# The first batch of a fused attention and feed-forward kernel: division by a product with diagonals, products with v in another PSUM bank, weight conversion moved behind the row maxima, and earlier starts of the feed-forward part

## The chip, the cores and the metric

The kernel runs on one core of one Trainium2 chip. The metric is the device time of one execution in microseconds. Times are medians of three or more executions. "The profile" is one profiled execution; its span is about 1.8 us shorter than the device time of the same execution.

In the lines of the profile PE is TensorE, PEld its weight loads, DVE VectorE, ACT ScalarE and POOL GpSimd. A line of a timeline gives the start and the length in us, the engine, the line of the kernel, the operation and its tiles; in brackets stands how long the engine was idle before it, and what ended that. A line of waits gives the total in us, the number of waits and the longest. The granted clock is the share of full speed that TensorE was given in a stretch. "To turn" weights means to transpose them in blocks of 128x128; the rest is the last 64 of the 576 keys.

## The reference, cut to what matters

```python
scores = scale * np.matmul(q, k.transpose(0, 1, 3, 2))        # 8 batches, 8 heads, 576 x 576
thresh = np.max(scores, axis=-1, keepdims=True) - tau
scores = np.where(scores >= thresh, scores, -1000000000.0)
attn = np.exp(scores - np.max(scores, axis=-1, keepdims=True))
attn = attn / (np.sum(attn, axis=-1, keepdims=True) + 1e-09)
attn_out = np.matmul(attn, v)                                 # -> x, 8 x 576 x 512
...
xn = (x - mu) / np.sqrt(var + 1e-06) * g_ln
out = x + np.maximum(xn @ w_ch1, 0.0) @ w_ch2                 # 512 -> 2048 -> 512
```

The two weight matrices arrive as 64-bit floats and are turned into 32-bit ones on the chip.

## The kernel before

The program issues 72 slots of attention, nine for each batch. A slot takes two heads and 256 of their 576 rows (the fifth slot takes the rest of all heads). Each slot has four quarters, at which pieces of other work are issued between the attention's own. Sixteen groups of 288 tokens go through the feed-forward part; the first can start when the first five slots are done.

Beside the first slots, 32 chunks of the weights are converted. One call of `tick` ends one chunk, carries the next, and begins a third. VectorE and ScalarE begin, GpSimd carries, VectorE ends.

```python
def tick(self):
    self.ticks += 1
    if self.ended < self.carried and self.due[self.ended] <= self.ticks:
        self.end()        # VectorE L266, then GpSimd L271 (scale by g)
    if self.carried < self.begun:
        self.carry()      # GpSimd L257
    if self.begun < self.fetched:
        self.begin()      # VectorE L239, L243; ScalarE L247, L251
```

The attention of a slot, with the division on GpSimd and, in the first batch, the turning on TensorE:

```python
def weights(es, thr):
    den = small.tile([128, 4], F32, tag="den", name="den")
    for i in range(4):
        nc.vector.scalar_tensor_tensor(                       # L389
            out=es[:, i], in0=blocks[i], scalar=thr[:, i : i + 1], in1=es[:, i],
            op0=ALU.is_ge, op1=ALU.mult, accum_out=den[:, i : i + 1],
        )
    nc.vector.reciprocal(den, den)
    for i in range(4):
        nc.gpsimd.tensor_scalar(                              # L395
            out=es[:, i], in0=es[:, i], scalar1=den[:, i : i + 1], scalar2=1.0, ...
        )

def turn_weights(s, es):
    em, er = turned_tiles(s)
    for i in range(4):
        if i == 2:
            yield
        tp = ps_ff.tile([128, J, 128], F32, tag="ff", name="tp")   # this pool has two PSUM buffers
        for c in range(J):
            nc.tensor.transpose(tp[:, c], es[:, i, c * 128 : (c + 1) * 128], ident)
        ...                                                   # ScalarE copies tp to em
    tr = ps_ff.tile([64, 4, 128], F32, tag="ff", name="tr")
    ...                                                       # the last 64 keys, copied to er
```

The loop over the slots, cut to the order of issue:

```python
pv = sc[0][:, 2 * S : 2 * S + QH]          # products with v: behind the scores, in their tile
...
for n in range(NS):
    b, s = divmod(n, SLOTS)
    ticks = (0, 2, 3) if n < 6 else range(5)
    tick(0)
    scores(b, s)                           # TensorE
    run(n, -1)                             # first half of turning the slot before
    rest = exponentials()                  # VectorE: maxima (L372); ScalarE: exponentials
    es, thr = next(rest)
    run(n, 0)                              # second half of turning
    ...
    tick(1); run(n, 1)
    weights(es, thr)
    tick(2); run(n, 2); tick(3)
    ...
    run(n, 3)                              # products with v of the slot before
    tick(4)
```

Of the kernel before, what the change touches and what calls it, by code (L numbers as in the profile page):

```python
# [8 lines left out]
F32 = mybir.dt.float32  # L9
# [9 lines left out]
def kernel(  # L19
# [31 lines left out]
    nc = tc.nc  # L51
    B, H, S, D = q.shape
# [3 lines left out]
    HP = H // 2  # L56
    NK = DM // 128
    ND = DF // 128
    J = 4
    NB = S // 32  # L60
    TOK = S // 2
    QH = 256
# [11 lines left out]
    ffn = ctx.enter_context(tc.tile_pool(name="ffn", bufs=2))  # L74
    ps_sc = ctx.enter_context(tc.tile_pool(name="ps_sc", bufs=1, space=bass.MemoryType.PSUM))
    ps_ff = ctx.enter_context(tc.tile_pool(name="ps_ff", bufs=2, space=bass.MemoryType.PSUM))
# [6 lines left out]
    ident = consts.tile([128, 128], F32, name="ident")  # L83
# [11 lines left out]
    def product(out, lhsT, rhs, **flags):  # L95


        for h in range(2):
            r = slice(64 * h, 64 * h + 64)
            nc.tensor.matmul(out[r], lhsT=lhsT[:, r], rhs=rhs, **flags)  # L100
# [20 lines left out]
    def load_v(u):  # L121
# [13 lines left out]
        out=tau_sb, in_=bass.AP(tensor=tau.tensor, offset=tau.offset, ap=[[0, 128], [1, 1]])  # L135
    )
    load_qk(0, (nc.sync, nc.scalar))
    for t in q_diag + rests + v_rest:
# [9 lines left out]
        out=scl_sb, in0=tau_sb, scalar1=0.0, scalar2=SCALE, op0=ALU.is_ge, op1=ALU.mult  # L148
    )
    nc.vector.tensor_scalar(  # L150
        out=low_sb, in0=tau_sb, scalar1=0.0, scalar2=BIG, op0=ALU.is_lt, op1=ALU.mult
    )
    nc.vector.scalar_tensor_tensor(
        out=low_sb, in0=tau_sb, scalar=-1.0, in1=low_sb, op0=ALU.mult, op1=ALU.subtract
# [5 lines left out]
    class Weights:  # L160
# [116 lines left out]
# [3 lines that stand above are left out]
                self.end()  # L280
            if self.carried < self.begun:
                self.carry()
            if self.begun < self.fetched:
                self.begin()

    def by_blocks(u):

        return units[u][0] > 0
# [33 lines left out]


    sc = [ps_sc.tile([128, 3 * 512], F32, name=f"sc{i}") for i in range(2)]
    pv = sc[0][:, 2 * S : 2 * S + QH]
    blocks = [sc[i // 2][:, i % 2 * S : i % 2 * S + S] for i in range(4)]

    def span(at, n):
# [53 lines left out]
                yield es, thr  # L382
            nc.scalar.activation(es[:, i], blocks[i], func=AF.Exp, bias=neg[:, i : i + 1])  # L383

    def weights(es, thr):

        den = small.tile([128, 4], F32, tag="den", name="den")
        for i in range(4):
            nc.vector.scalar_tensor_tensor(  # L389
                out=es[:, i], in0=blocks[i], scalar=thr[:, i : i + 1], in1=es[:, i],  # L390
                op0=ALU.is_ge, op1=ALU.mult, accum_out=den[:, i : i + 1],
            )
        nc.vector.reciprocal(den, den)  # L393
        for i in range(4):
            nc.gpsimd.tensor_scalar(  # L395
                out=es[:, i], in0=es[:, i], scalar1=den[:, i : i + 1], scalar2=1.0,
                op0=ALU.mult, op1=ALU.mult,
            )



# [3 lines left out]
    def turned_tiles(s):  # L405
        return att.tile([128, J, 4, 128], F32, tag="em", bufs=1, name="em"), rests[s % 2]

    def turn_weights(s, es):

        em, er = turned_tiles(s)  # L410
        for i in range(4):
            if i == 2:
                yield
            tp = ps_ff.tile([128, J, 128], F32, tag="ff", name="tp")
            for c in range(J):
                nc.tensor.transpose(tp[:, c], es[:, i, c * 128 : (c + 1) * 128], ident)
            if s == HP:
                nc.scalar.copy(
                    em[:, :, :, 32 * i : 32 * i + 32], tp.rearrange("p c (a x) -> p c a x", a=4)
                )  # L420
            else:
                h, j = divmod(i, 2)
                nc.scalar.copy(  # L423
                    em[:, :, 2 * j : 2 * j + 2, 64 * h : 64 * h + 64],
                    tp.rearrange("p c (a x) -> p c a x", a=2),
                )
        tr = ps_ff.tile([64, 4, 128], F32, tag="ff", name="tr")
        for i in range(4):
            nc.tensor.transpose(tr[:, i], es[:, i, 512:576], ident)  # L429
        if s == HP:  # L430
            nc.scalar.copy(
                er[:64].rearrange("p a (u x) -> p u a x", u=HP),
                tr.rearrange("p u (a x) -> p u a x", a=4),
            )
        else:
            nc.scalar.copy(
                er[:64].rearrange("p a (h x) -> p h a x", h=2),
                tr.rearrange("p (h j) (a x) -> p h (j a) x", h=2, a=2),
            )
        yield em, er  # L440
# [38 lines left out]
    def values_of(b, s, turned_weights):  # L479

        em, er = turned_weights
        if s == HP:
            outs = [(hp, pv[:, hp * 64 : hp * 64 + 64]) for hp in range(HP)]
            pick = lambda t, hp, h: t[:, 2 * h : 2 * h + 2, hp * 32 : hp * 32 + 32]
        else:
            outs = [(s if s < HP else s - HP - 1, pv)]
            pick = lambda t, hp, h: t[:, :, 64 * h : 64 * h + 64]
        for hp, dst in outs:
            vt, vr = values_in[b * HP + hp]
            for c in range(J + 1):  # L490
                for h in range(2):
                    nc.tensor.matmul(  # L492
                        dst[64 * h : 64 * h + 64],
                        lhsT=vt[:, c, h, :] if c < J else vr[:, h, :],
                        rhs=pick(em[:, c] if c < J else er, hp, h),
                        start=(c == 0), stop=(c == J),
                    )
        if s == HP:
            for t in range(2):
                nc.scalar.copy(  # L500
                    x_of(2 * b + t)[:, :, QH:],
                    pv.rearrange("p (u t x) -> p t u x", u=HP, t=2)[:, t],
                )
                for c in range(1, NK):
                    add_feature(2 * b + t, c, slice(QH, TOK))
        else:
            g = 2 * b + (s > HP)
            hp = outs[0][0]
            nc.scalar.copy(x_of(g)[:, hp, :QH], pv)  # L509
            if hp:  # L510
                add_feature(g, hp, slice(0, QH))
# [30 lines left out]
    def run_all(calls):  # L542
        now = calls[:]
        calls.clear()
        for fn in now:
            fn()
# [79 lines left out]
    def at_quarter(n, i, fn, *args):  # L626
        later_calls.setdefault((n, i), []).append((fn, args))
# [4 lines left out]

    def ready(g):

        b, t = divmod(g, 2)
        return QUARTERS * (b * SLOTS + (HP, 2 * HP)[t] + 2) + (2, 4)[t]

# [42 lines left out]
    load_v(1)  # L680
    for n in range(NS):
        b, s = divmod(n, SLOTS)
        ticks = (0, 2, 3) if n < 6 else range(5)

        def tick(i):
            if i in ticks:
                conversion.tick()

        tick(0)
        scores(b, s)  # L690
        run(n, -1)
        rest = exponentials()
        es, thr = next(rest)
        run(n, 0)
        conversion.fetch(2)
        run_all(stores)
        second_part(n, 0)
        next(rest, None)

        u = (n + 1) // SLOTS * HP + (n + 1) % SLOTS  # L700
        if (n + 1) % SLOTS < HP and u < len(units):
            turn(u)
            if u + 1 < len(units):
                load_qk(u + 1)
        run_all(aside)
        tick(1)
        run(n, 1)
        second_part(n, 1)
        weights(es, thr)
        run_all(aside)  # L710
        run_all(stores)
        tick(2)
        run(n, 2)
        second_part(n, 2)
        tick(3)
        box = []
        if by_blocks(b * HP):
            scr = turn_blocks(s, es)
            at_quarter(n + 1, 0, lambda s=s, scr=scr, box=box: box.append(fetch(s, scr)))
        else:  # L720
            made = turn_weights(s, es)
            at_quarter(n + 1, -1, next, made)
            at_quarter(n + 1, 0, lambda made=made, box=box: box.append(next(made)))
        at_quarter(n + 1, 3, lambda b=b, s=s, box=box: values_of(b, s, box[0]))
        if s in (HP, 2 * HP):
            group_ready(2 * b + (s > HP))
        run_all(aside)
        conversion.fetch(2)
        run(n, 3)
        if b == 0 and s < HP - 2:  # L730
            load_v(s + 2)
        elif n >= SLOTS - 2 and (n + 2) % SLOTS < HP and n < NS - 2:
            load_v((n + 2) // SLOTS * HP + (n + 2) % SLOTS)
        second_part(n, 3)
        tick(4)
        run_all(aside)
    while later_calls or queue or aside or stores:
        n += 1
        for i in range(QUARTERS):
            run(n, i)  # L740
            second_part(n, i)
            run_all(aside)
            run_all(stores)
# [30 lines left out]
```

## Time and profile before

The time before is 1529.1 us (four executions, 1528.78 to 1529.36). The stretches of the span:

| stretch, us | TensorE busy, us | granted clock |
|---|---|---|
| 0 to 30 | 9.54 | 0.77 |
| 30 to 134 (attention of slots 1 to 6 and conversion) | 56.45 of 104 | 0.75 |
| 134 to 212 (slots 6 to 9, first feed-forward group) | 65.59 of 78 | 0.87 |
| 212 to 290 | 75.52 of 78 | 0.99 |

After that TensorE is busy at full clock nearly all the time.

### The profile page before, as it was taken

The page shows a single profiled execution, that of the slowest core. Times are in us where ns is not written, and L with a number is a line of the kernel's source. Part 1 is how long each engine was busy: PE and PEld are TensorE (multiplying, and loading weights), DVE is VectorE, ACT ScalarE, POOL GpSimd, SP SyncE. Part 2 cuts the span into 40 slices and gives each one's busy share as a digit, 9 for nine tenths or more (in the row PEclk, how much of TensorE's full clock was granted, in tenths as well). Part 3 has the DMA queues.
Part 4 walks back from the last instruction along what each step waited for, and adds up shares of the span by engine and source line. Part 5 has one row for each costly group of instructions (what it writes and reads, how often), then busy time and mean ns, then how long its engine had stood idle before and what let it go on. Part 6 is the DMA issues. An engine that isn't in the chain of part 4 may idle for free.

```text
span 1527.7 us, 28886 instructions
## 1 busy us (share of the span) xinstructions
PE 1416.8 (93%) x11700; PEld 833.7 (55%) x11700; DVE 837.7 (55%) x1380; ACT 442.2 (29%) x797; POOL 487.7 (32%) x737
## 2 busy tenths in 40 slices
PE   3557899999999999999999999999999999999998
PEld 1335455565555555565555655565555655565554
DVE  5877855555654566455664556455654556545210
ACT  3445531323132322314132232313222231313120
POOL 4667443222332323132331323223232323222100
PEclk8777899999999999999999999999999999999999
DMA  9611237455764577555774567645774567545300
GB/s 221 163 39 57 68 82 165 120 136 149 173 164 125 135 171 176 135 137 148 170 169 118 147 154 175 153 125 138 160 169 125 145 152 174 141 125 136 101 9 16
DMA packets 460693, 205.07 MB, mean 134 GB/s; under 512 B 275024, under 2 KB 420176, under 8 KB 460560
## 3 DMA queue, kind: packets, MB, share of 16 engines
q1 hardware_dynamic: 458160, 202.93, 54.4%
q8 instruction: 92, 1.51, 0.4%
q10 hardware_dynamic: 2368, 0.30, 0.2%
q14 instruction: 41, 0.34, 0.1%
q0 software_dynamic: 32, 0.00, 0.0%
HBM read 119.41 MB, written 83.76 MB: 133 GB/s over the span
## 4 chain that ended last, share of the span: by engine, by line
PE 83%; ACT 5%; DVE 5%; POOL 2%; issue 2%; SPq 1%; DMA 1%; POOLq 0%; ACTq 0%; DVEq 0%
PE p L100 62%; PE sc L492 10%; PE sc L359 8%; ACT e L383 4%; DVE neg L372 3%; PE sc L100 2%; POOL e L395 1%; DVE e L389 1%; SPq L112 1%; ACT hidden L587 1%; PE mean L100 1%; ACT L383 0%; DMA v_rest<-in_v_dram 0%; ACT em L423 0%; PE tr L429 0%
## 5 line engine op out<-in xcount | busy, mean ns | idle before, releaser
L100 PE MATMUL p<-xc,w 128*64 128x288 f32 x4096 | 528.5, 414 | 24.9 <-ACT hidden L587 23.6
L100 PE MATMUL p<-hidden,w 128*64 128x288 f32 x4096 | 514.2, 407 | 0.0
L100 PEld LDWEIGHTS p<-xc,w 128*64 128x64 f32 x4096 | 293.5, 139 | 239.5 <-ACT hidden L587 39.0
L100 PEld LDWEIGHTS p<-hidden,w 128*64 128x64 f32 x4096 | 291.2, 137 | 198.4 <-issue 1.4
L372 DVE TENSOR_REDUCE neg<-sc 128x2 f32<-128x1152 f32 x144 | 189.4, 1352 | 339.8 <-PE sc L359 270.0
L395 POOL TENSOR_SCALAR e<-e,den 128x576 f32<-128x576 f32 x288 | 227.3, 806 | 282.9 <-DVE den L393 263.1
L383 ACT ACTIVATE e<-sc,neg 128x576 f32<-128x576 f32 x288 | 192.7, 742 | 289.0 <-DVE neg L372 272.1
L389 DVE SCALAR_TENSOR_TENSOR e<-sc,thr,e 128x576 f32<-128x576 f32 x288 | 219.1, 813 | 26.7 <-ACT e L383 26.2
L453 DVE STREAM_TRANSPOSE et<-e 128x1152 f32<-128x1152 f32 x112 | 153.1, 1372 | 72.5 <-POOL e L395 61.5
L587 ACT ACTIVATE hidden<-p 128x288 f32<-128x288 f32 x256 | 105.1, 415 | 278.2 <-PE p L100 276.1
L359 PE MATMUL sc<-kT,qT 64*128 64x512 f32 (+3 forms) x1024 | 154.3, 439 | 22.7 <-DVE e L389 10.9
L376 POOL TENSOR_SCALAR thr<-neg,low_sb 128x2 f32<-128x2 f32 x144 | 40.3, 280 | 374.2 <-DVE neg L372 374.2
L492 PE MATMUL sc<-em,v_in 128*64 128x256 f32 (+1 forms) x1536 | 149.1, 340 | 4.8 <-DVE e L389 4.4
L359 PEld LDWEIGHTS sc<-kT,qT 64*128 64x128 f32 x1024 | 86.1, 191 | 106.2 <-issue 79.9
L492 PEld LDWEIGHTS sc<-em,v_in 128*64 128x64 f32 x1536 | 97.4, 144 | 49.2 <-DVE e L389 7.1
L509 ACT COPY x<-sc 128x256 f32<-128x256 f32 x64 | 23.9, 373 | 320.5 <-PE sc L492 320.4
L550 DVE TENSOR_TENSOR o<-p,rb 128x288 f32<-128x288 f32 x64 | 28.3, 442 | 123.1 <-PE p L100 123.1
L551 POOL TENSOR_TENSOR o<-o,x 128x288 f32<-128x288 f32 x64 | 51.1, 798 | 131.6 <-DVE o L550 131.3
L518 POOL TENSOR_TENSOR sum<-sum,x 128x256 f32<-128x256 f32 (+1 forms) x64 | 32.2, 502 | 108.2 <-ACT x L509 105.7
L593 POOL TENSOR_TENSOR sq<-sq 128x288 f32<-128x288 f32 x48 | 38.7, 807 | 45.8 <-ACT sq L591 43.3
L492 PE MATMUL sc<-rest,v_rest 128*64 128x256 f32 (+1 forms) x384 | 49.3, 336 | 0.0
L599 DVE RECIPROCAL rb<-rb 128x288 f32<-128x288 f32 x16 | 31.2, 1953 | 30.3 <-ACT rb L598 29.9
(107 smaller groups left out, 656.1 us busy)
## 6 DMA issues: line engine op xcount, KB each, us to landing
scr<-et SPq DMA_DIRECT2D x252, 288.0 KB, 5.1
em<-scr SPq DMA_DIRECT2D x63, 1024.0 KB, 5.9
q_in<-in_q_dram SPq DMA_DIRECT2D x128, 72.0 KB, 3.4
out_dram<-ot SPq DMA_DIRECT2D x256, 36.0 KB, 4.1
k_in<-in_k_dram SPq DMA_DIRECT2D x124, 72.0 KB, 2.7
v_in<-in_v_dram SPq DMA_DIRECT2D x64, 128.0 KB, 4.3
rest<-scr SPq DMA_DIRECT2D x63, 128.0 KB, 5.9
w<-in_moe_w_ch_dram SPq DMA_DIRECT2D x12, 512.0 KB, 4.8
```

The costliest lines, as they stand in the source:

```text
L100: nc.tensor.matmul(out[r], lhsT=lhsT[:, r], rhs=rhs, **flags)
L359: nc.tensor.matmul(sc[h][:, at : at + n], lhsT=qT[r, half, j * 128 : (j + 1) * 128], rhs=kT[r, o : o + n], start=True, stop=True,)
L372: nc.vector.tensor_reduce(out=neg[:, i], in_=sc[h][:, : 2 * S].rearrange("p (j n) -> p j n", j=2), axis=AXL.X, op=ALU.max, negate=True,)
L376: nc.gpsimd.tensor_scalar(out=thr[:, i], in0=neg[:, i], scalar1=-1.0, scalar2=low_sb, op0=ALU.mult, op1=ALU.add,)
L383: nc.scalar.activation(es[:, i], blocks[i], func=AF.Exp, bias=neg[:, i : i + 1])
L389: nc.vector.scalar_tensor_tensor(out=es[:, i], in0=blocks[i], scalar=thr[:, i : i + 1], in1=es[:, i], op0=ALU.is_ge, op1=ALU.mult, accum_o ...
L395: nc.gpsimd.tensor_scalar(out=es[:, i], in0=es[:, i], scalar1=den[:, i : i + 1], scalar2=1.0, op0=ALU.mult, op1=ALU.mult,)
L453: nc.vector.transpose(et[:, :, 64 * h : 64 * h + 64].rearrange("p n (j c) -> p j n c", j=2), es[:, 2 * h : 2 * h + 2].rearrange("p j (n c) ...
L492: nc.tensor.matmul(dst[64 * h : 64 * h + 64], lhsT=vt[:, c, h, :] if c < J else vr[:, h, :], rhs=pick(em[:, c] if c < J else er, hp, h), s ...
L551: nc.gpsimd.tensor_tensor(out=o, in0=o, in1=groups[g][:, m], op=ALU.add)
L587: nc.scalar.activation(hidden[:, d], p1, func=AF.Relu)
L593: nc.gpsimd.tensor_tensor(out=sq[:, 0], in0=sq[:, 0], in1=sq[:, c], op=ALU.add)
```

## The change

The intent is to shorten the slots of the first batch, so that the feed-forward part starts sooner. It has four parts. GpSimd no longer divides the weights: it multiplies the identity by the reciprocals, and TensorE's product with that diagonal turns and divides at once. The products with v go to a buffer of the two-buffer pool, a quarter earlier. The ticks move behind the maxima, three to four in the first six slots and six afterwards. The first two groups start at earlier quarters.

```diff
-    pv = sc[0][:, 2 * S : 2 * S + QH]
+    pv_behind = sc[0][:, 2 * S : 2 * S + QH]
...
+        diags = []
         for i in range(4):
+            if divide:
+                src = dst = es[:, i]
+            else:
+                if i % 2 == 0:
+                    two = ffn.tile([128, TOK], F32, tag="o", bufs=6, name="diag")
+                src, dst = ident, two[:, i % 2 * 128 : i % 2 * 128 + 128]
+                diags.append(dst)
             nc.gpsimd.tensor_scalar(
-                out=es[:, i], in0=es[:, i], scalar1=den[:, i : i + 1], scalar2=1.0,
+                out=dst, in0=src, scalar1=den[:, i : i + 1], scalar2=1.0,
...
-                nc.tensor.transpose(tp[:, c], es[:, i, c * 128 : (c + 1) * 128], ident)
+                product(
+                    tp[:, c], lhsT=es[:, i, c * 128 : (c + 1) * 128], rhs=diags[i],
+                    start=True, stop=True,
+                )
...
+        pv = pv_behind
+        if b == 0 and s <= HP:
+            pv = ps_ff.tile([128, QH], F32, tag="ff", name="pv")
...
     def ready(g):
+        if g < 2:
+            return (24, 41)[g]           # 26 and 44 before
...
-        ticks = (0, 2, 3) if n < 6 else range(5)
+        ticks = range(1, 4 + n // 3) if n < 6 else range(6)
...
-        at_quarter(n + 1, 3, lambda b=b, s=s, box=box: values_of(b, s, box[0]))
+        at_quarter(
+            n + 1, 2 if b == 0 and s <= HP else 3,
+            lambda b=b, s=s, box=box: values_of(b, s, box[0]),
+        )
```

`product` issues two half products of 64 columns each. In the changed kernel the line numbers differ: L389 becomes L390, L395 L404, L416 L100 (inside `product`), L423 L437 and L429 L443.

More of the change, by code (lines that the diff above doesn't have):

```diff
@@ L383, in exponentials, with weights @@
             nc.scalar.activation(es[:, i], blocks[i], func=AF.Exp, bias=neg[:, i : i + 1])
-    def weights(es, thr):
+    def weights(es, thr, divide):
         den = small.tile([128, 4], F32, tag="den", name="den")
@@ L393, in weights, with turn_weights @@
         nc.vector.reciprocal(den, den)
+        diags = []
         for i in range(4):
+            if divide:
[5 more added lines that the diff above has]
+                diags.append(dst)
             nc.gpsimd.tensor_scalar(
-                out=es[:, i], in0=es[:, i], scalar1=den[:, i : i + 1], scalar2=1.0,
+                out=dst, in0=src, scalar1=den[:, i : i + 1], scalar2=1.0,
                 op0=ALU.mult, op1=ALU.mult,
             )
+        return diags
     def turned_tiles(s):
         return att.tile([128, J, 4, 128], F32, tag="em", bufs=1, name="em"), rests[s % 2]
-    def turn_weights(s, es):
+    def turn_weights(s, es, diags):
         em, er = turned_tiles(s)
@@ L428, in turn_weights @@
         for i in range(4):
-            nc.tensor.transpose(tr[:, i], es[:, i, 512:576], ident)
+            nc.tensor.matmul(
+                tr[:, i], lhsT=es[:, i, J * 128 :], rhs=diags[i], start=True, stop=True
+            )
         if s == HP:
@@ L708 @@
         second_part(n, 1)
-        weights(es, thr)
+        blocks_go = by_blocks(b * HP)
+        diags = weights(es, thr, blocks_go)
         run_all(aside)
@@ L716 @@
         box = []
-        if by_blocks(b * HP):
+        if blocks_go:
             scr = turn_blocks(s, es)
@@ L720 @@
         else:
-            made = turn_weights(s, es)
+            made = turn_weights(s, es, diags)
             at_quarter(n + 1, -1, next, made)
             at_quarter(n + 1, 0, lambda made=made, box=box: box.append(next(made)))
-        at_quarter(n + 1, 3, lambda b=b, s=s, box=box: values_of(b, s, box[0]))
+        at_quarter(
+            n + 1, 2 if b == 0 and s <= HP else 3,
+            lambda b=b, s=s, box=box: values_of(b, s, box[0]),
+        )
         if s in (HP, 2 * HP):
@@ L736 @@
         run_all(aside)
+        tick(5)
     while later_calls or queue or aside or stores:
```

## The prediction

> **What bounds the kernel now.** I first read the busy shares of the whole span and the 40 slices of 38.2 us, to see whether one engine is the bound everywhere.
>
> ```profile
> PE 1416.8 (93%) x11700; PEld 833.7 (55%) x11700; DVE 837.7 (55%) x1380; ACT 442.2 (29%) x797; POOL 487.7 (32%) x737
> ...
> PE   3557899999999999999999999999999999999998
> ...
> DVE  5877855555654566455664556455654556545210
> ...
> PEclk8777899999999999999999999999999999999999
> ```
>
> TensorE is the bound from the sixth slice on; before that VectorE is busier and TensorE's clock is lower. So the change, which touches the first batch alone, can only win back idle TensorE time at the start. I then asked for busy times by stretch: TensorE is busy 9.5 of the first 30 us, 56.5 of 104 us (30 to 134), 65.6 of 78 us (134 to 212) and 75.5 of 78 us (212 to 290). Idle until 290: 83 us. That is the ceiling.
>
> The first batch is nine slots of attention (one pair of heads each), beside which 32 chunks of the feed-forward weights are converted. I call one step of that conversion a tick: VectorE ends one chunk (L266) and begins another (L239, L243), and GpSimd scales (L271) and carries (L257). A slot can be measured from one row maximum (L372) to the next: 53.56, 72.49, 91.35, 110.21, 128.67, 153.85, so 18.9 us each while attention runs alone. The timeline of VectorE and GpSimd for one of them says why:
>
> ```profile
> 61.65 0.66 DVE L266 SCALAR_TENSOR_TENSOR hidden<-hidden 128x512 f32<-128x512 f32 x1
> ...
> 61.91 4.98 POOL L395 TENSOR_SCALAR e<-e,den 128x576 f32<-128x576 f32 x4 [4.64 <-DVE den L393]
> ...
> 67.53 1.29 POOL L257 TENSOR_TENSOR hidden<-hidden,w 128x512 int32<-128x512 int32 x1
> ...
> 68.85 1.18 DVE L266 SCALAR_TENSOR_TENSOR hidden<-hidden 128x512 f32<-128x512 f32 x1 [2.58 <-POOL hidden L257]
> 69.95 1.50 DVE L239 TENSOR_SCALAR hidden<-et 128x512 uint32<-128x512 uint32 x1
> ```
>
> GpSimd divides the weights for 5 us; the carry behind it comes late; VectorE waits 2.58 us for it, and only then gets to the next maxima. Also, VectorE's same operation lasts 0.66 us or 1.18, and 0.42 or 1.50, the long ones beside GpSimd's L257. VectorE is busy 15.7 of 18.9 us, so it is nearly the bound itself. TensorE waits behind that:
>
> ```profile
> PE tr L429 <- ACT em L423: 23.9, 5, 6.1
> ```
>
> This line of the waits between 30 and 134 us blames ScalarE's copies, but these stand in order behind exponentials that wait for the maxima.
>
> **What the Trainium skill says.** GPSIMD Engine Reference, section 2 (Architecture): GpSimd's SBUF port is shared with VectorE. The 0.66/1.18 and 0.42/1.50 us pairs agree. TensorE: Matmul & The Clock Gate, Terms: a transpose mode is four times faster for fp32. The trace has a transposed 128x128 block at 0.15 us (four in 0.60) against 0.48 us for a 128x288 fp32 product, which at width 128 would be 0.21: the same direction, a smaller ratio. The same page, Part 1 (the clock gate): the array runs at half clock until it has been busy for about 3.4 us. The trace agrees: after its 5.3 us wait at 157.1 TensorE needs 12.10 us for 78 matmuls that take 9.95 us at the later 0.1275 us each, 2.1 us lost.
>
> **The change, part by part.**
>
> 1. Division. Removed from GpSimd per slot: four 128x576 multiplications, 4.98 us. Added: four 128x128 ones on the identity. No row has this shape; from 0.28 us for 128x2 and 0.81 for 128x576 I interpolate 0.40, so 1.6 us. GpSimd saves 3.4 us per slot, more than the 2.58 us that VectorE waits.
>
> 2. Order. A tick goes from before the maxima to behind them, where it covers the exponentials (VectorE waits 0.26 + 1.90 us for ScalarE in the slot at 72.49). Ticks go from three to four in slots 3 to 5, and from five to six later. The order of instructions shows four ticks between maxima in slots 3 and 4, and five plus the centring in slot 5.
>
> A tick costs VectorE 2.75 us now (61.65 to 72.49, less the wait, over three). VectorE's own new slots: maxima 2.63, turning q and k 2.3 (where done), weights 3.17, plus ticks. Slots 1 and 2: 2.63 + 2.3 + 3.17 + 8.25 = 16.35. Slots 3 and 4: 2.63 + 3.17 + 11.0 = 16.8. Slot 5: 2.63 + 3.17 + 13.75 + 1.6 = 21.15. Slot 0: the maxima of slot 1 come now at 34.64; without the wait and the end behind it, near 31.2. So slot 6's maxima fall at 31.2 + 32.7 + 33.6 + 21.15 = 118.7 instead of 128.67. Less collision with GpSimd may make ticks 2.5 us: 20 x 0.25 = 5 us more. Gain by slot 6: 10 to 15 us.
>
> 3. Feed-forward start. Now its first product starts at 134.83, and slot 6 holds 16 of its steps. In the new order slot 6 holds 32, starting right behind the last turned rest, some 4.3 us after the maxima: 123. TensorE becomes the bound at once: 32 x 0.51 = 16.3, products with v 2.2, scores 2.3, turning 4.1 + 1.0. So slot 7's steps start near 123 + 26 + 1.5 (cold clock) = 150.5 instead of 158.13, with 16 x 0.51 = 8.1 us more behind them. Sum so far 15.7 us; in slots 7 and 8 about 1 us each as idle (2.8 and 3.3 us now, before the rest is turned) is filled. About 17.5 us.
>
> 4. Price on TensorE. 16 transposes of 0.15 us become 64 instructions of half products: 3.4 us by width, or 4.1 us if weight loads bound them (59 ns each in the 64-wide products of slot 4). So +1.7 us per slot; idle time covers it until slot 6, and three slots are charged in the sums above.
>
> 5. Products with v in a free bank. Now they wait for the weights (L389), 4.4 us in two waits, and the next scores wait for x. That shifts TensorE's work earlier by 2 us in slots where TensorE waits for VectorE anyway: 0.
>
> 6. Thinner filling. The first group's end moves from quarter 44 to 41, the second keeps 62, so its work spreads over 21 quarters instead of 18. TensorE waits 23.6 us in 21 pieces for ScalarE's hidden rows between 212 us and the end; with less work per slot I charge 2 us.
>
> Sum: 17.5 - 2 = 15.5, and half of the possible 5 us of shorter ticks: 18 us. 1529 - 18 = 1511.
>
> **Rivals.** (a) VectorE stays the bound: with more ticks per slot it has 16.4 to 21 us of work, ticks stay at 2.75 or lengthen because GpSimd's L257 still runs beside them, and 0.42/1.50 shows how strongly. Then the gain is 10 us: 1519. (b) The new products become the wait: at half clock they take twice 3.4 us, ScalarE's copies come late and the exponentials behind them hold up VectorE. I placed them from the reciprocal R: scores until R + 2.7, turning until R + 9.5, the rest copied at R + 12, second exponentials at R + 13; VectorE wants them at R + 14.7. It fits by less than 2 us; if not, each of slots 1 to 5 loses about 2 us: 1521. (c) The chunks come late: with ticks used up sooner, a transfer (one took the queue 5.5 us at 63.67) could starve them. The order of buffers looks safe: 1518. (d) All works and the clock stays up: lost half-clock time of 2.1 us in each of slots 6, 7 and 8 comes back, ticks shrink to 2.3: 1502. More than 30.6 us, needed for 2%, would take over a third of the ceiling, and the loads of the first 30 us are untouched.
>
> **Range and chances.** 1511, and 1501 to 1521 covers (a) to (d) nearly. Faster by over 2% (below 1498.6) needs (d) and more: 0.06. Slower by over 2% has no mechanism: 0.01. Within 2%: 0.93.
>
> **What would show it.** Right: slots of 16 to 17 us between maxima from slot 1; VectorE's wait for L257 near 0 there; four divisions in 1.6 us; slot 6's maxima at 113 to 119; the first feed-forward product at 118 to 124; TensorE's idle time until 290 us down from 83 to about 70. Step 3 is wrong if TensorE idles over 3 us in slot 6; step 4 if turning takes over 5 us at full clock; step 6 if TensorE idles clearly more than now between 212 and 330. The total is wrong above all if VectorE's ticks don't keep to 2.5 to 2.75 us.

## More of the kernel before

VectorE's waits for the carries between 30 and 134 us are 15.4 us in all:

```profile
DVE w L266 <- POOL w L257: 7.7, 3, 2.6
DVE hidden L266 <- POOL hidden L257: 7.7, 3, 2.6
```

## The result, and the profile after

The changed kernel takes 1512.14 us (median of four, 1509.87 to 1514.95) against 1529.1 us. The ratio is 0.989, with a 95% interval of 0.9869 to 0.9911. The gain is real and lies within 2%. The profiled execution was one of the faster ones: its span is 1508.4 us against 1527.7 us, 19.3 us less.

The page of the changed kernel (busy shares, then busy tenths in 40 slices of 37.7 us):

```profile
PE 1423.0 (94%) x12168; PEld 861.2 (57%) x12168; DVE 822.3 (55%) x1380; ACT 442.6 (29%) x797; POOL 470.5 (31%) x737
...
PE   4859999999999999999999999999999999999998
...
DVE  5877646555645555455655556455564556455210
...
PEclk8879999999999999999999999999999999999999
```

TensorE reaches its full state in the fourth slice instead of the sixth, and its clock is at 9 from the fourth slice on. Its busy time went up by 6.2 us, not down: the change adds work to the engine that bounds the kernel and still wins.

Busy time of each engine by stretch, of the kernel before and then of the changed one. The columns are the stretch, its length, busy microseconds with the number of instructions for TensorE, its weight loads, VectorE, ScalarE and GpSimd, then granted clock, DMA share and GB/s:

```profile
30.00:134.00 104.00, 56.45 (x382) 36.60 (x380) 81.06 (x118) 50.03 (x90) 73.72 (x79) 0.75 0.38 108
134.00:212.00 78.00, 65.59 (x458) 38.36 (x456) 56.32 (x88) 41.36 (x75) 40.54 (x39) 0.87 0.23 64
212.00:290.00 78.00, 75.52 (x608) 43.62 (x608) 41.54 (x73) 19.53 (x36) 23.24 (x34) 0.99 0.63 144
```

```profile
30.00:134.00 104.00, 77.56 (x778) 61.80 (x777) 84.84 (x145) 59.94 (x107) 74.93 (x84) 0.85 0.40 118
134.00:212.00 78.00, 71.35 (x674) 51.01 (x672) 45.32 (x76) 34.38 (x61) 28.60 (x39) 1.00 0.25 61
212.00:290.00 78.00, 77.45 (x636) 45.00 (x634) 43.68 (x72) 22.80 (x41) 22.50 (x36) 1.00 0.63 151
```

Until 290 us TensorE's idle time falls from 82.9 to 55.1 us. Of these 27.8 us the turning takes 17.8: transposes and rests are busy for 30.8 us before, products and rests for 48.6 us after. The clock between 134 and 212 us goes from 0.87 to 1.00, so the busy time there also holds more work. The mean of the third group falls at 312.56 us instead of 331.59, 19.0 us earlier, and the end is 19.3 us earlier. So in these two executions all of the gain is made at the start, and nothing is given back later.

The slots can be read from the starts of their maxima on VectorE:

| maxima of slot | 1 | 2 | 3 | 4 | 5 | 6 |
|---|---|---|---|---|---|---|
| before | 34.64 | 53.56 | 72.49 | 91.35 | 110.21 | 128.67 |
| predicted | 31.2 | 47.6 | 63.9 | 80.7 | 97.5 | 118.7 |
| after | 30.89 | 44.61 | 60.41 | 79.81 | 96.95 | 120.12 |

The end agrees and the way there doesn't: slots 1 and 2 are shorter than predicted, and slots 3 and 5 are longer. Lines of the timeline of the changed kernel, slot 1 (start, length, engine, line, operation), that answer to those shown of before:

```profile
41.16 0.66 DVE L266 SCALAR_TENSOR_TENSOR w<-w 128x512 f32<-128x512 f32 x1
41.34 3.60 POOL L404 TENSOR_SCALAR diag<-ident,den 128x128 f32<-128x128 f32 x4 [2.12 <-DVE den L394]
...
42.19 0.69 DVE L243 SCALAR_TENSOR_TENSOR hidden<-w,hidden 128x512 uint32<-128x512 uint32 x1
42.80 0.69 DVE L266 SCALAR_TENSOR_TENSOR w<-w 128x512 f32<-128x512 f32 x1
...
44.61 2.61 DVE L372 TENSOR_REDUCE neg<-sc 128x2 f32<-128x1152 f32 x2
```

VectorE does its two ticks at their short lengths and is at the next maxima 3.6 us after the reciprocal (at 41.06), before GpSimd has even made its carry (at 45.57). There is no wait between. The surprise is the second line: the four small multiplications take 3.60 us, where I had interpolated 1.6.

In slot 3 the turning at a low clock and, later, the carry of the fourth tick are the waits:

```profile
60.41 2.62 DVE L372 TENSOR_REDUCE neg<-sc 128x2 f32<-128x1152 f32 x2 [0.44 <-PE sc L359]
...
60.71 5.60 PE L100 MATMUL tp<-diag,e 128*64 128x128 f32 x64
...
64.44 0.59 ACT L437 COPY em<-tp 128x512 f32<-128x512 f32 x1 [1.07 <-PE tp L100]
64.92 1.38 ACT L383 ACTIVATE e<-sc,neg 128x576 f32<-128x576 f32 x2
...
69.90 0.82 DVE L390 SCALAR_TENSOR_TENSOR e<-sc,thr,e 128x576 f32<-128x576 f32 x1 [1.93 <-ACT e L383]
...
77.34 1.20 DVE L266 SCALAR_TENSOR_TENSOR hidden<-hidden 128x512 f32<-128x512 f32 x1 [2.20 <-POOL hidden L257]
```

The first maxima are there at 61.8, but ScalarE's exponentials stand behind its copies of turned weights, and these wait for products that take 5.60 us (granted clock 0.61 between 54 and 67 us; the next turning, at 1.00, takes 3.90 us). The second pair of exponentials comes behind the rest, so VectorE waits 1.93 us more at 69.90. The fourth tick of the slot then waits 2.20 us for its carry, as that of slot 4 does. These two waits are all that is left of the 15.4 us:

```profile
DVE hidden L266 <- POOL hidden L257: 2.2, 1, 2.2
DVE et L266 <- POOL et L257: 2.2, 1, 2.2
```

In slot 5 something else waits:

```profile
106.15 3.51 POOL L404 TENSOR_SCALAR diag<-ident,den 128x128 f32<-128x128 f32 x4 [2.44 <-DVE den L394]
...
112.49 1.23 PE L100 MATMUL mean<-sum,avg_sb 128*64 128x288 f32 x4 [6.33 <-POOL sum L537]
...
113.84 1.55 DVE L552 TENSOR_TENSOR xc<-x,mean 128x288 f32<-128x288 f32 x4 [4.42 <-PE mean L100]
```

The sums for the first group stand behind the diagonals and a carry on GpSimd; the mean waits for them, and VectorE waits 4.42 us for the mean.

### The profile page after: what moved, and what is told of

Its sections match the earlier page's. It is cut to its first block, busy times and chain, and to the rows that moved or that the text cites. A ratio compares the mean times of both kernels' runs of the same rounds, so it can differ in the third digit from the quotient of the medians.

```text
span 1508.4 us, 29807 instructions
## 1 busy us (share of the span) xinstructions
PE 1423.0 (94%) x12168; PEld 861.2 (57%) x12168; DVE 822.3 (55%) x1380; ACT 442.6 (29%) x797; POOL 470.5 (31%) x737
## 4 chain that ended last, share of the span: by engine, by line
PE 85%; ACT 6%; DVE 4%; SPq 1%; issue 1%; POOL 1%; DMA 1%; POOLq 0%; ACTq 0%; DVEq 0%
PE p L100 62%; PE sc L511 10%; PE sc L359 9%; ACT e L383 4%; DVE neg L372 2%; PE sc L100 2%; SPq L112 1%; ACT hidden L606 1%; PE tp L100 1%; DMA v_rest<-in_v_dram 1%; POOL diag L404 1%; PE tr L443 1%; ACT L383 1%; PE mean L100 1%; DVE e L390 0%
## 5 line engine op out<-in xcount | busy, mean ns | idle before, releaser
L100 PE MATMUL p<-xc,w 128*64 128x288 f32 x4096 | 520.6, 409 | 24.7 <-ACT hidden L606 24.1
L100 PE MATMUL p<-hidden,w 128*64 128x288 f32 x4096 | 513.6, 407 | 0.2 <-ACT rest L452 0.2
L100 PEld LDWEIGHTS p<-xc,w 128*64 128x64 f32 x4096 | 296.2, 137 | 227.5 <-ACT hidden L606 39.9
L100 PEld LDWEIGHTS p<-hidden,w 128*64 128x64 f32 x4096 | 293.3, 137 | 195.5 <-ACT rest L452 0.7
L404 POOL TENSOR_SCALAR e<-e,den 128x576 f32<-128x576 f32 x252 | 183.6, 746 | 231.3 <-DVE den L394 226.4
L390 DVE SCALAR_TENSOR_TENSOR e<-sc,thr,e 128x576 f32<-128x576 f32 x288 | 219.1, 813 | 20.1 <-ACT e L383 19.4
L469 DVE STREAM_TRANSPOSE et<-e 128x1152 f32<-128x1152 f32 x112 | 153.2, 1372 | 72.8 <-POOL e L404 61.8
L359 PE MATMUL sc<-kT,qT 64*128 64x64 f32 (+3 forms) x1024 | 159.5, 445 | 27.0 <-DVE e L390 16.8
L511 PE MATMUL sc<-em,v_in 128*64 128x256 f32 (+1 forms) x1408 | 130.8, 329 | 1.8 <-DVE o L569 1.8
L511 PEld LDWEIGHTS sc<-em,v_in 128*64 128x64 f32 x1408 | 86.1, 137 | 40.3 <-DVE o L569 2.3
L618 DVE RECIPROCAL rb<-rb 128x288 f32<-128x288 f32 x16 | 31.2, 1950 | 35.3 <-ACT rb L617 35.0
L511 PE MATMUL sc<-rest,v_rest 128*64 128x256 f32 (+1 forms) x352 | 44.5, 329 | 0.0
```

What stands on the lines that cost most here:

```text
L100: nc.tensor.matmul(out[r], lhsT=lhsT[:, r], rhs=rhs, **flags)
L359: nc.tensor.matmul(sc[h][:, at : at + n], lhsT=qT[r, half, j * 128 : (j + 1) * 128], rhs=kT[r, o : o + n], start=True, stop=True,)
L390: nc.vector.scalar_tensor_tensor(out=es[:, i], in0=blocks[i], scalar=thr[:, i : i + 1], in1=es[:, i], op0=ALU.is_ge, op1=ALU.mult, accum_o ...
L404: nc.gpsimd.tensor_scalar(out=dst, in0=src, scalar1=den[:, i : i + 1], scalar2=1.0, op0=ALU.mult, op1=ALU.mult,)
L469: nc.vector.transpose(et[:, :, 64 * h : 64 * h + 64].rearrange("p n (j c) -> p j n c", j=2), es[:, 2 * h : 2 * h + 2].rearrange("p j (n c) ...
L511: nc.tensor.matmul(dst[64 * h : 64 * h + 64], lhsT=vt[:, c, h, :] if c < J else vr[:, h, :], rhs=pick(em[:, c] if c < J else er, hp, h), s ...
```

## The experiments

Twelve runs were made, in four jobs on four chips. Each job ran the kernel before on the same chip (medians 1528.54 to 1529.49 us). Only the first job ran the changed kernel too; runs of the others are compared with it across chips. Edits are against the changed kernel unless said otherwise, cut, and with comments added. The starting theory was that of the prediction: VectorE sets the slots, and both the division and the order of the ticks take waits from it. The rivals were that one of the two brings all, that the products cost more than thought, and that the earlier start is the gain. The last column is the start of the maxima of slot 6 in the profiled execution, in us.

| run | what | median us | ratio to before, 95% interval | maxima of slot 6 |
|---|---|---|---|---|
| (result) | changed kernel | 1512.14 | 0.9890, 0.9869 to 0.9911 | 120.12 |
| after_again | changed kernel | 1513.05 | 0.9905, 0.9888 to 0.9922 | 120.23 |
| a_fulldiv | division undone | 1516.60 | 0.9922, 0.9907 to 0.9937 | 123.66 |
| a_oldticks | ticks undone | 1522.80 | 0.9960, 0.9945 to 0.9975 | 123.15 |
| a_oldready | starts undone | 1519.48 | 0.9942, 0.9927 to 0.9956 | 119.83 |
| a_pvbehind | bank undone | 1514.95 | 0.9907, 0.9891 to 0.9924 | 122.17 |
| b_ticks | ticks alone | 1523.22 | 0.9968, 0.9953 to 0.9983 | 121.85 |
| b_div | division alone | 1521.88 | 0.9959, 0.9944 to 0.9973 | 123.29 |
| a_transp_wrong | transposes, diagonals unused | 1508.70 | 0.9871, 0.9857 to 0.9886 | 116.46 |
| a_latemean | mean and centring later | 1513.15 | 0.9900, 0.9884 to 0.9917 | 118.97 |
| a_3ticks | three ticks in slots 3 to 5 | 1503.86 | 0.9837, 0.9822 to 0.9853 | 110.40 |
| a_actdiv | division on ScalarE | 1510.35 | 0.9877, 0.9860 to 0.9895 | 113.06 |
| a_actdiv_3ticks | both of these | 1501.61 | 0.9817, 0.9803 to 0.9830 | 106.08 |

### The changed kernel again

No edit.

> The changed kernel once more, as the yardstick of this job. Four runs so far fell into two groups (1510 and 1514.5 us). If that spread belongs to the chip and not to the execution, the three runs here agree within 1 us; if it belongs to the execution, they spread over some 5 us again.

The four executions took 1510.22, 1512.15, 1513.94 and 1516.81 us, on one chip. So the spread belongs to the execution. The kernel before spread by 3 us in the same rounds. I did not find what makes the executions of the changed kernel differ. Their mean granted clocks (0.982, 0.981, 0.980, 0.979) fall as the times rise, but in the first four executions the slowest (1514.95 us) has the highest clock (0.987). The ratios are not always those of all listed executions either: for this run all four give 0.9898, and for the last run of the table all five give 0.9823. Differences below some 3 us in the table are therefore read from the slots, not from the medians alone.

### The division undone

```diff
-            if divide:
+            if True:                      # GpSimd divides 128x576 four times
...
-                product(tp[:, c], lhsT=es[:, i, ...], rhs=diags[i], start=True, stop=True)
+                nc.tensor.transpose(tp[:, c], es[:, i, ...], ident)
```

(and the same for the rest of 64 keys)

> The changed kernel with the division put back: GpSimd divides 128x576 four times and TensorE transposes against the identity; order, ticks, bank and starts stay changed. Theory (the division delays the carry and lengthens VectorE's operations beside it): slots 1 to 5 each 2 to 3 us longer, VectorE's wait for L257 back at 2 us or more per slot, time 8 to 12 us above after_again. Rival (the order and the earlier start bring the gain, the division nothing): within 3 us of after_again. Second rival (the products on TensorE cost more than the division saved): up to 5 us faster than after_again.

It is 3.5 us slower, and the intervals of the ratios overlap; in the trace the maxima of slot 6 come 3.4 us later. So neither the theory (8 to 12 us) nor the rival (within 3 us) is hit squarely; it lies close to the rival. VectorE's waits for L257 between 30 and 134 us are two, of 2.6 us each, against two of 2.2 us in the changed kernel: in the new order the carry has the maxima and the exponentials between it and the end of its chunk, whoever divides. What the small division still brings is shorter ticks: L239, L243 and L266 together cost 2.34 us per tick here and 2.12 in the changed kernel (mean of each line between 30 and 108 us, summed).

### The ticks undone

```diff
-        ticks = range(1, 4 + n // 3) if n < 6 else range(6)
+        ticks = (0, 2, 3) if n < 6 else range(5)
```

> The changed kernel with the old ticks (before the maxima, three in each of the first six slots, then five). Theory: the carry is no longer late, so a tick ahead of the maxima costs only the cover of the exponentials, about 2 us in slots 3 to 5, and one tick fewer in slots 3 to 5 gives 2 us each back; slot 6 starts no later; but conversion ends later and the second half of the first group waits for chunks: 2 to 6 us above after_again. Rival (moving the ticks is the main gain): 10 us or more above.

It is 9.8 us slower, close to the rival that the order is the main gain. The theory failed already in the first slots: it had the carry no longer late, but VectorE's waits for L257 between 30 and 134 us are 10.7 us, with the small division in place:

```profile
DVE hidden L266 <- POOL hidden L257: 6.6, 3, 2.2
DVE w L266 <- POOL w L257: 4.1, 2, 2.2
```

The maxima of slot 6 are only 2.9 us later, with one tick fewer in each of slots 3 to 5. The effect of the place alone can be read against the run with three ticks below: until slot 6 the two kernels differ only in where the three ticks of each slot stand, and there the maxima of slot 6 fall at 110.40 instead of 123.15, 12.8 us earlier, with no wait for L257 before slot 6. The rest is lost later: there were fewer ticks, and the conversion ends in slot 9 instead of slot 8. TensorE's timeline shows it at the end:

```profile
203.54 2.13 PE L100 MATMUL p<-hidden,w 128*64 128x288 f32 x7
208.08 1.23 PE L100 MATMUL p<-hidden,w 128*64 128x288 f32 x4 [2.41 <-DVE w L266]
```

A feed-forward product waits 2.41 us for the end of a chunk. In the same stretch, 186 to 212 us, turned blocks wait 3.8 us for ScalarE's copies (1.5 us in the changed kernel between 120 and 230), and TensorE is busy for 18.66 of 26 us at clock 0.77 (22.27 at 1.00 in the changed kernel). So the ticks are worth two things: the place of each, and their number by slot 8; no run changes the number after slot 5 alone.

### The starts undone

```diff
-        if g < 2:
-            return (24, 41)[g]
```

> The changed kernel with the old starts of the first two groups (quarters 26 and 44 instead of 24 and 41). Theory: TensorE's idle time in slot 6 comes back, since the feed-forward starts half a slot later: 6 to 8 us of its work (half of 32 steps at 0.51 us) moves behind, so 5 to 8 us above after_again. Rival (the pacing only moves work about, TensorE being the bound anyway from slot 6): within 2 us.

It is 6.4 us slower, as the theory had it. The maxima of slot 6 fall at 119.83, as early as in the changed kernel, but TensorE has less to do in slot 6: it waits 12.8 us before turned rests between 120 and 230 us (4.4 us in the changed kernel), and its clock is 0.87 between 134 and 160 us instead of 1.00. Without the earlier starts the other three parts win 9.2 of 15.6 us (medians of this job).

### The products with v behind the scores again

```diff
-        if b == 0 and s <= HP:
-            pv = ps_ff.tile([128, QH], F32, tag="ff", name="pv")
...
-            n + 1, 2 if b == 0 and s <= HP else 3,
+            n + 1, 3,
```

> The changed kernel with the products with v back in the bank behind the scores, and back at quarter 3. Theory (TensorE waits for VectorE there anyway): within 2 us of the changed kernel. Rival (the values then wait for the weights, the next scores for x, and with shorter slots the maxima wait for the scores): the slots 1 to 4 longer by 1 us or more each, 4 us or more above.

The median is 1.9 us above the changed kernel and the intervals overlap; slot 1 takes 16.5 us instead of 13.7, slot 3 takes 18.4 instead of 19.4, and the maxima of slot 6 are 2.0 us later. That is just inside the theory's 2 us and far from the rival's 4 or more: a small gain, not a proven one.

### The ticks alone

```diff
-        ticks = (0, 2, 3) if n < 6 else range(5)
+        ticks = range(1, 4 + n // 3) if n < 6 else range(6)
...
         tick(4)
         run_all(aside)
+        tick(5)
```

(on the kernel before)

> The kernel before with the new ticks alone (behind the maxima; three, then four, then six); the division on GpSimd, the bank and the starts as before. The runs so far say that undoing the ticks costs 10 us and undoing the division 3.5 us. Theory (the order removes the wait for the carry by itself, since a carry that comes late now has the maxima and exponentials between it and the end of its chunk): VectorE's waits for L257 between 30 and 134 us fall below 5 us (15.4 before) and slots 1 to 5 shrink by 1 to 3 us; 1519 to 1523. Rival (the order pays only with the small division): 1526 or more.

It gains 5.7 us at the medians; 1523.22 us is just outside the theory's 1519 to 1523, and below the rival's 1526. The waits for L257 fall from 15.4 to 7.8 us (three of 2.6 us), more than the 5 us that I expected. Slots 3 to 5 are no shorter than before (20.0, 18.8 and 19.8 us) but hold a tick more each.

### The division alone

```diff
-        if b == 0 and s <= HP:
-            pv = ps_ff.tile([128, QH], F32, tag="ff", name="pv")
...
-        if g < 2:
-            return (24, 41)[g]
...
-        ticks = range(1, 4 + n // 3) if n < 6 else range(6)
+        ticks = (0, 2, 3) if n < 6 else range(5)
...
-            n + 1, 2 if b == 0 and s <= HP else 3,
+            n + 1, 3,
```

(on the changed kernel: diagonals and products stay; bank, starts and ticks are those of before)

> The kernel before with the division by products alone; ticks, bank and starts as before. Theory: in the old order the third end of each slot waits for a carry that stands behind the division; four divisions take 3.5 us instead of 5.0, so 1.5 us of the 2.6 us wait goes, plus about 0.3 us per tick of collision; five slots, 1.5 to 2.5 us each: 8 to 12 us less until slot 6, of which products that TensorE pays in slots 6 to 8 take 3: 1520 to 1524. Rival (the division is worth as little here as in the new order): 1525 to 1528.

It gains 7.0 us, inside the theory's 5 to 9 us. The maxima of slot 6 come 5.4 us earlier, slots take 17.4 to 18.3 us instead of 18.9, and a tick costs 2.55 us instead of 2.79 (means as above). The waits for L257 fall only from 15.4 to 12.8 us, so the wait that the division was to take mostly stays; the larger part of the 5.4 us goes with the shorter ticks (about 4 us, an estimate: 0.24 us for each of some 17). The division is worth about twice as much in the old order as in the new. The parts are not additive: alone they give 5.7 and 7.0 us, and undone they cost 9.8 and 3.5 us. Nor is the start: this run, with the old starts and bank, takes 1521.88 us, and a_oldticks, with the new ones, 1522.80. Without the new ticks the earlier starts and the bank bring nothing that can be measured; with them the starts bring 6.4 us.

### Transposes with the diagonals unused

```diff
-                product(tp[:, c], lhsT=es[:, i, ...], rhs=diags[i], start=True, stop=True)
+                nc.tensor.transpose(tp[:, c], es[:, i, ...], ident)     # not divided: wrong on purpose
```

> The changed kernel with the diagonals still made by GpSimd but not used: TensorE transposes the undivided weights against the identity. The result is wrong on purpose; every other engine's instructions are the same. It measures what the products cost against the transposes. Theory (at half clock the products take 5.6 us and ScalarE's copies, the exponentials behind them and so VectorE wait, above all in slot 3): slot 3 falls from 19.4 to about 17 us, and three slots of TensorE's own work are 1.7 us each cheaper: 4 to 7 us faster than the changed kernel. Rival (the products lie in TensorE's idle time): within 2 us.

The result is wrong, as meant (relative error 0.37). It takes 1508.70 us, 4.3 us less than the changed kernel, inside the theory's range. In the profiled execution the maxima of slot 6 fall at 116.46, 3.8 us earlier than in after_again, and the lead is not clearly larger later (2.4 us at slot 7, 3.5 at slot 8, 4.4 at 310 us). So nearly all is lost before slot 6, where I had written that idle time covers the products. Slot 3 in this run:

```profile
60.71 3.81 PE L427 MATMUL tp<-ident,e 128*128 128x128 f32 x16
63.19 1.38 ACT L383 ACTIVATE e<-sc,neg 128x576 f32<-128x576 f32 x2
...
68.14 0.82 DVE L390 SCALAR_TENSOR_TENSOR e<-sc,thr,e 128x576 f32<-128x576 f32 x1 [0.50 <-ACT e L383]
...
78.04 2.61 DVE L372 TENSOR_REDUCE neg<-sc 128x2 f32<-128x1152 f32 x2
```

Turning starts at the same 60.71, the exponentials start 1.7 us earlier, VectorE waits 0.50 us instead of 1.93, and the next maxima come at 78.04 instead of 79.81.

### Mean and centring later

```diff
-        for fn in (mean_of, centre):
-            at_quarter(*divmod(at, QUARTERS), fn, g)
+        if g == 0:
+            at_quarter(HP + 2, -1, mean_of, g)      # behind the scores of slot 6
+            at_quarter(HP + 2, 0, centre, g)        # behind its maxima
+        else: ...
```

> The changed kernel with the first group's mean behind the scores of slot 6 on TensorE, and its centring behind the maxima of slot 6 on VectorE. In the changed kernel VectorE waits 4.4 us in slot 5 for the mean, which waits for sums that stand behind diagonals and carries on GpSimd. Theory (VectorE's chain to the maxima of slot 6 sets the start of the feed-forward): the wait goes, maxima of slot 6 near 116 instead of 120.1, 3 to 4.5 us faster than the changed kernel. Rival (scores or turning take the wait's place, or the centring behind the maxima is as late): within 1.5 us.

Nothing was gained (1513.15 us): the rival, though by a mechanism I had not named. VectorE's 4.4 us wait is gone, but TensorE's timeline shows a new one:

```profile
112.53 1.23 PE L100 MATMUL mean<-sum,avg_sb 128*64 128x288 f32 x4 [4.60 <-POOL sum L537]
113.54 1.92 PE L100 MATMUL tp<-diag,e 128*64 128x128 f32 x16
...
116.15 1.98 PE L100 MATMUL tp<-diag,e 128*64 128x128 f32 x16 [0.69 <-ACT em L437]
...
121.50 1.54 DVE L552 TENSOR_TENSOR xc<-x,mean 128x288 f32<-128x288 f32 x4
...
122.25 1.97 PE L100 MATMUL tp<-diag,e 128*64 128x128 f32 x16 [1.47 <-ACT em L437]
```

The mean now stays in one of the pool's two PSUM buffers until the centring at 121.50. The turning has a single buffer left, so each block waits for ScalarE's copy of the one before, 2.9 us in three waits. It runs from 113.5 to 124.2, and the feed-forward starts at 125.3 instead of 124.1. The buffer is not the whole of it: the four blocks are busy for 7.9 us instead of 3.75, at granted clock 0.50 between 113.5 and 124.2 (1.00 between 117 and 121 in the changed kernel). Here TensorE's 4.60 us wait for the sums comes right before the turning, where in the changed kernel the scores lie between. No run separates the two.

### Three ticks in slots 3 to 5

```diff
-        ticks = range(1, 4 + n // 3) if n < 6 else range(6)
+        ticks = range(1, 4) if n < 6 else range(6)
```

> The changed kernel with three ticks instead of four in slots 3 to 5. Theory (VectorE is the bound until slot 6, and the feed-forward needs only a few chunks at first): each of slots 3 to 5 shorter by a tick of 2.2 us less new waits for ScalarE, slot 6 at about 115; but the conversion ends half a slot later, and the second half of the first group waits for chunks: 2 to 4 us faster. Rival (ScalarE's exponentials behind the turning set these slots, not VectorE): within 1.5 us, or slower.

It takes 1503.86 us, 9 us less than the changed kernel and more than I expected. The maxima of slot 6 come at 110.40, 9.7 us earlier. Slots 3 and 4 are shorter by 4.8 and 4.2 us, more than a tick: with the fourth tick its 2.20 us wait for the carry is gone too. Slot 5 is shorter by only 0.7 us; its wait of 4.4 us for the mean stays. So slots 3 and 4 were indeed VectorE's, and the later end of the conversion costs nothing that shows: between 110 and 300 us TensorE has no wait for the end of a chunk among its five longest causes. This is the plainest sign that the fourth tick was one too many there: it delayed the start for chunks that the start didn't need.

### Division on ScalarE

```diff
+            if not divide:
+                nc.scalar.activation(es[:, i], es[:, i], func=AF.Copy, scale=den[:, i : i + 1])
+                continue
...
-                product(tp[:, c], lhsT=es[:, i, ...], rhs=diags[i], start=True, stop=True)
+                nc.tensor.transpose(tp[:, c], es[:, i, ...], ident)
```

> The changed kernel with the first batch's division on ScalarE (four 128x576 copies with a scale for each row) and transposes on TensorE; no diagonals, GpSimd has no division in batch one. The run with unused diagonals and transposes took 1508.7 us with GpSimd's 3.5 us per slot still there. Theory (products cost 4.3 us, and GpSimd's diagonals collide with VectorE's ticks): 1504 to 1509. Rival (ScalarE is filled: its 3 us per slot delay its part of the conversion, the copies and the exponentials): 1513 or more.

The transposes replace the products here too. It takes 1510.35 us, between theory and rival. The maxima of slot 6 come at 113.06, 7 us earlier than in the changed kernel. But TensorE then waits 5.4 us for ScalarE's hidden rows between 120 and 230 us (1.8 us in the changed kernel), and the median is only 2.7 us below that of after_again. So more than half of the lead is lost again; that ScalarE, now with the division, takes it is my reading of these waits.

### Both

> The two variants that were faster than the changed kernel, together: division on ScalarE with transposes on TensorE (1510.4 us alone), and three ticks in slots 3 to 5 (1503.9 us alone). Theory (VectorE sets the slots until slot 6 in both, so what each takes from it adds): maxima of slot 6 near 107, 1499 to 1503 us. Rival (with three ticks ScalarE or the turning sets slots 3 to 5, and ScalarE has 3 us more to do in each): 1503 to 1508 us, no better than three ticks alone.

The edits are those of the last two runs. It takes 1501.61 us (five executions), with a correct result, 27.9 us below the kernel before in its rounds and inside the theory's 1499 to 1503 us. The ratio 0.9817 against 0.9837 for three ticks alone leaves the intervals overlapping, so that it beats three ticks alone is likely and not shown. Both are faster than the changed kernel, whose intervals theirs don't touch.

## Why the prediction was right

The predicted time, 1511 us with a range of 1501 to 1521, holds the measured 1512.1. The place of the gain was right: only time until 290 us, with the rest of the span shifted as a whole. But some steps behind the sum missed in opposite directions, and of the six signs that were to show it right none came out as written: slots of 13.7, 15.8, 19.4, 17.1 and 23.2 us instead of 16 to 17; waits for L257 of 4.4 us, not near 0; four divisions in 3.5 us, not 1.6; the maxima of slot 6 at 120.12 and the first feed-forward product at 124.11, each just past its range; idle time of 55.1 us, not about 70. Of the signs of being wrong, TensorE's idle time in slot 6 (2.7 us) and the turning at full clock (3.9 us) stayed within bounds, and the ticks did not keep to 2.5 to 2.75 us.

**Step 1, the division.** The interpolated 0.40 us for a 128x128 multiplication was wrong where it counts. GpSimd takes 0.88 us each (3.51 us for four in slots 3 and 5), so it saves 1.5 us per slot and not 3.4. In the trace the same four take 1.69 us where VectorE has only one L266 beside their start:

```profile
182.73 1.69 POOL L404 TENSOR_SCALAR diag<-ident,den 128x128 f32<-128x128 f32 x4 [6.36 <-DVE den L394]
```

So about 0.42 us is the length of one nearly alone. Beside one tick four take 2.40 us (at 160.99) and beside two 3.51 to 3.60, while VectorE's operations beside them keep their short lengths (0.66, 0.42 and 0.69 us at 41.16 to 42.19): here the collision costs GpSimd. I had read it on VectorE's side only, and put it down to L257 alone; the L266 of 1.18 us at 68.85 runs mostly beside an L271 (68.80 to 69.49). And the step credited the division with the 2.58 us wait. The waits for L257 say otherwise: 15.4 us before, 12.8 with the division alone, 7.8 with the ticks alone, 4.4 in the changed kernel. It was the order that took most of that wait.

**Step 2, the order.** Right in kind and the larger part: 9.8 us when undone, place and number of the ticks together. A tick costs 2.12 us (2.79 before, by the same means), below my 2.75 and even below the 2.5 that I called possible. By the table of slots that made slots 1 and 2 shorter by 2.6 and 0.6 us than predicted; in slot 2 VectorE waits 2.15 us for q_in from GpSimd (at 50.06), which the sum left out. More such waits took the rest back: in slot 3 (19.4 us against 16.8) 1.93 us behind the turning and 2.20 for the carry, in slot 4 the carry again, and in slot 5 the wait of 4.42 us for the mean, which made the slot 23.2 us against 21.15.

**Step 3, the feed-forward start.** The first product was predicted at 123 and came at 124.11; the steps of slot 7 were predicted at 150.5 and came at 149.5. The run with the old starts shows the size of this part: 6.4 us.

**Step 4, the price on TensorE.** The term was about right in size (4.3 us measured; three slots of 1.7 us charged) and wrong in place. "Idle time covers it until slot 6" failed: by the traces nearly all of it is lost before slot 6. Rival (b) had the mechanism, and with "it fits by less than 2 us" I had come close to seeing that it wouldn't.

**Step 5, the bank.** Predicted 0; measured 1.9 us with overlapping intervals. It stays open whether it is above 0.

**Step 6, thinner filling.** The 2 us charged did not appear as a loss: the lead is 19.0 us at 312 us and 19.3 at the end, and TensorE was busier than before between 212 and 290 us. Its waits for ScalarE's hidden rows from 212 us on are 22.3 us, against 23.6 before.

**Idle time.** I wrote that idle time until 290 us would fall to about 70 us. It fell to 55.1, because the added products fill idle time as well. Idle time was the wrong thing to write down; the start of a later group is the cleaner mark.

So the number was right in part by luck: shorter ticks (too much cost assumed) paid for the waits in slots 2 to 5 (no cost assumed).

## What to carry to other kernels

When an engine that prepares work for the bounding one is itself nearly full, ask first where in its order each piece stands and whether the start needs that piece at all. Undoing the new ticks cost 9.8 us, and leaving out one tick in each of slots 3 to 5 gained another 9, while making the neighbouring engine's work four and a half times narrower was worth 3.5. Before a result in a small PSUM pool is kept longer to remove a wait, count the buffers left to the others. And price an operation of GpSimd from rows taken beside the same VectorE work, not from the mean over the whole span: the 0.81 us that I interpolated from was the span's mean, and the same rows took 1.25 us in the slot that I showed. Even that would have given only about 0.5 us (an estimate by the same interpolation), where 0.88 was measured.

## What the Trainium skill lacked or had wrong

- GPSIMD Engine Reference, section 2 (Architecture), says that the SBUF port is shared with VectorE and gives no price there; what other pages say of the sharing was not compared. In these runs four 128x128 multiplications take 1.69 us where VectorE runs hardly anything of a tick and 3.51 us beside its ticks, and VectorE's L239 takes 0.42 us or up to 1.5 us.
- TensorE: Matmul & The Clock Gate, Terms, gives the transpose mode as four times faster for fp32. In this kernel, at granted clock 1.00, 16 blocks turned by products take 3.90 us in a row, and by transposes two runs of eight take 1.10 and 1.14 us: a ratio of 1.7. The products here are split into two of 64 columns, each with its own weight load, so this is not a measure of the mode alone.
- No page of the skill that I read says what holding one of two PSUM buffers costs: the blocks of one slot's turning waited 2.9 us for copies in three waits when the mean kept the second buffer (none between the blocks before).
